# Top-32 attention and two feed-forward layers on one core: scores rewritten in place, divisions and norms moved to ScalarE, early heads parked in DRAM, and a new order

## The chip, the cores and the metric

One NeuronCore of one Trainium2 chip runs the whole program. The metric is device time of one execution in microseconds (us); lower is better. The engines are TensorE (PE; PEld is its weight load), VectorE (DVE), ScalarE (ACT), GpSimd (POOL) and SyncE (SP), which issues every DMA of this kernel from one in-order queue.

## The reference, cut to what matters

```python
B, H, S, D = 4, 8, 576, 64                 # attention; then d_model = 512, hidden 2048
scores = q @ k.T / sqrt(D)                 # per batch and head, 576 x 576
kth = 32nd largest score of each row
attn = softmax(scores where scores >= kth, else -1e9)
x = (attn @ v), heads side by side         # (4, 576, 512)

u = x + real(fft over seq of fft over d_model of x)
u = u + relu(norm(u) @ w_ch1) @ w_ch2      # first feed-forward (w1a, w2a in the kernel)
out = u + relu((norm(u) * g_ln) @ w_ch1') @ w_ch2'   # second feed-forward (w1b, w2b)
```

Inputs are float32; the kernel splits float32 operands into pairs of float16 (high part, low part) and multiplies high*high, high*low, low*high, so each product of the feed-forward layers is three matmuls.

## The kernel before

**Tiles.** A *score tile* is 128 query rows by 576 keys. Each of the 4 batches has 36 of them: 8 heads with 4 tiles each, and 4 tiles that hold the last 64 rows of two heads, 144 in all. The function `attend` makes one: matmuls into `ps`, a ScalarE copy to `s`, then on VectorE four `MAX8` (the eight largest of each row) with three `MATCH_REPLACE8` between them (each with a `MATCH_VALUE_LOAD`), which leaves the 32nd largest score in `mx`. Then ScalarE makes the masked exponential (Prelu with a huge slope, then Exp), rounds it to float16 (`p`), GpSimd writes the low part beside it, a DMA transposes `p` to `pt`, and 14 matmuls multiply it with the values `vt` into `xp`. After the four tiles of a head `evacuate` divides by the sum of the weights and writes the head's columns into the batch's buffers `xA` and `xB` (and `xC` for the 64-row tiles). `xp` is one buffer: the next head's products wait until it is emptied.

**A batch after its attention.** `fourier_rows` (once after heads 0, 7, 1, 6, once at the end) and `fourier_columns` add the transform to `xA`, `xB`, `xC`; `norm` takes mean and variance on VectorE, a power on GpSimd, applies them (`t2k<-xA,tiny`), and a DMA transposes the float16 pair into `unT`. `ffn` then runs 16 steps for two row tiles (A or B, 256 rows) or one (C, shared by two batches): 12 matmuls of 256 columns with `W1A` or `W1B` into `mm`, a ReLU into `h`, and 6 matmuls per pair of row tiles of 512 columns into `acc`. The second layer's `w2b` comes from DRAM (`ws<-W2D`), step by step. At the end `xA`, `xB`, `xC` go out; B goes through two DMA transposes and a GpSimd copy that turn its rows round.

**Buffers.** `xA` and `xB` exist twice, so batch 2 can write its first head only when batch 0 has left the second feed-forward and its rows are on their way out; batch 3 waits for batch 1 in the same way. `s` exists three times, the exponential `e` twice, the scratch `t2k` three times.

**Weights and statistics.** The weights arrive as 64-bit words and are converted on ScalarE, VectorE and GpSimd (`W1A`, `W2A`, `W2F`, `W1B`), scaled by a power of two and split. `stats(b)` loads q, k and v of batch b piece by piece, lets TensorE form sums of squares, and `find_scales` makes the batch's scales `sc`, without which `prep` (load, scale, split, transpose q and k) can't begin. Batch 0's scores are computed in float32.

**What sets the order.** `Program.record` only notes operations. `Program.order` then places them: it keeps a clock for each engine and takes again and again the operation that can start first by the prices of `price`; among operations that could start alike the lower priority number wins. That number is `LEVELS[stage][engine]`, a table with five numbers for each named stage (`st`, `a`, `p`, `f`, `m`, `n`, `w...`), and then the order of writing. `PACE` gives the earliest times of loads of weights and statistics. The result is a fixed order for each engine and a fixed buffer for each tile; on the chip each engine works through its list in that order and waits where it must. The scheduler emits everything on one line, so all rows of the profile have line 427.

The batch loop sets stage names around `stats(b+1)`, `attention(b+1)`, `first_ffn(b, ...)`, `front(b+1)` and `second_ffn(b, ...)`: the feed-forward layers of batch b are mixed with the attention of batch b+1 wherever the planner sees room.

## Time and profile before

| | us |
|---|---|
| median of 3 runs (lowest to highest) | 1364.93 (1363.99 to 1368.43) |
| the profiled execution | 1367.71 |
| its span, first to last instruction | 1365.9 |
| TensorE busy | 1196.4 (88%) |
| VectorE busy | 1028.4 (75%) |
| ScalarE busy | 796.2 (58%) |
| GpSimd busy | 676.6 (50%) |
| weight loads on TensorE (PEld) | 749.4 (55%) |
| mean granted TensorE clock | 0.939 of full speed |

Busy times count an engine's instructions, neighbours overlap a little. An instruction's duration in the trace is longer than its share of the engine's time: the next one starts before it has ended. Where a cost is taken from a timeline, it is the distance between two starts. Matmul ends are modelled, so a stretch in which TensorE is busy isn't one in which it runs at its peak.

### The profile page before, as it was taken

To read this page: it belongs to the slowest core of one execution; us is meant where nothing else is said; L and a number is where in the kernel's file an instruction comes from. 1 tells how busy PE (TensorE), PEld (TensorE's weight loads), DVE (VectorE), ACT (ScalarE), POOL (GpSimd) and SP (SyncE) were. 2 spreads that over 40 slices of the span, in tenths; PEclk is the share of its full clock that TensorE was granted. 3 is DMA by queue.
4 is the path that set the end of the run, shared out by engine and by line. 5 is a ranking of instruction groups with operands and counts; after the bars stand their busy time and mean duration, and the time that the engine had idled before them with its cause. 6 is when DMAs were issued, how large, how long until landed. Compare 5 with 4: busy or idle time off the path is not lost. (4 is left out here: it accounts for less than half of the span.)

```text
span 1365.9 us, 27326 instructions
## 1 busy us (share of the span) xinstructions
PE 1196.4 (88%) x9422; PEld 749.4 (55%) x9422; DVE 1028.4 (75%) x2597; ACT 796.2 (58%) x1741; POOL 676.6 (50%) x1015
## 2 busy tenths in 40 slices
PE   6787887577788779989999999979999999999995
PEld 3343434333555446656666666656666666666663
DVE  5989898978999898499599996968999751322221
ACT  3569696577786986466667664667676541212111
POOL 3566344545786874576667546656664441101000
PEclk9998787578899979999999999999999999999999
DMA  6898637767866457777454675895545735002346
GB/s 176 228 269 217 165 76 237 188 179 184 202 145 138 86 107 171 198 140 166 96 111 73 122 154 117 192 203 113 97 78 102 163 77 120 17 9 70 116 108 155
DMA packets 349430, 190.11 MB, mean 139 GB/s; under 512 B 288617, under 2 KB 306154, under 8 KB 349162
## 3 DMA queue, kind: packets, MB, share of 16 engines
q1 hardware_dynamic: 349290, 188.35, 59.5%
q8 instruction: 74, 1.21, 0.4%
q14 instruction: 66, 0.54, 0.1%
HBM read 108.07 MB, written 13.11 MB: 89 GB/s over the span
## 5 line engine op out<-in xcount | busy, mean ns | idle before, releaser
L427 DVE MAX8 mx<-w 128x8 f32<-128x576 f32 x432 | 315.6, 748 | 2.4
L427 ACT ACTIVATE h<-mm 128x256 f16<-128x256 f32 (+1 forms) x320 | 114.7, 358 | 307.7 <-PE mm L427 250.6
L427 POOL TENSOR_TENSOR p<-e,p 128x512 f16<-128x512 f32 (+1 forms) x288 | 207.4, 738 | 96.1 <-ACT p L427 76.9
L427 PEld LDWEIGHTS <-h 128*128 128x128 f16 x1728 | 160.6, 98 | 161.1 <-issue 26.3
L427 PE MATMUL acc<-ws,h 128*128 128x512 f16 x864 | 223.3, 383 | 18.1 <-DMA ws<-W2D 17.5
L427 PE MATMUL mm<-unT,W1B 128*128 128x256 f16 (+1 forms) x1920 | 225.0, 264 | 10.7 <-ACT W1B L427 5.4
L427 PE MATMUL mm<-unT,W1A 128*128 128x256 f16 (+1 forms) x1920 | 226.1, 264 | 2.9 <-DMA unT<-t2k 2.8
L427 PE MATMUL acc<-W2A,h 128*128 128x512 f16 x864 | 221.5, 380 | 5.1 <-POOL h L427 2.9
L427 POOL TENSOR_TENSOR h<-hr,h 128x256 f16<-128x256 f32 (+1 forms) x224 | 143.2, 642 | 151.1 <-ACT hr L427 76.0
L427 PEld LDWEIGHTS <-W1B 128*128 128x128 f16 (+1 forms) x1984 | 177.4, 99 | 72.8 <-issue 10.0
L427 PEld LDWEIGHTS <-W1A 128*128 128x128 f16 (+1 forms) x1984 | 178.2, 99 | 70.0 <-POOL W1A L427 10.6
L427 DVE MATCH_REPLACE8 w<-mx,w 128x576 f32<-128x576 f32 x288 | 213.0, 740 | 0.0
L427 DVE SCALAR_TENSOR_TENSOR h<-mm,h 128x256 f16<-128x256 f32 (+1 forms) x96 | 36.3, 378 | 166.5 <-ACT h L427 146.7
L427 ACT ACTIVATE e<-s,tiny 128x576 f32<-128x576 f32 x144 | 110.6, 774 | 60.3 <-DVE tiny L427 58.3
L427 PEld LDWEIGHTS <-pt 128*128 128x128 f16 (+1 forms) x2240 | 95.7, 106 | 70.3 <-DMA pt<-p 43.7
L427 PE MATMUL xp<-vt,pt 128*128 128x65 f16 (+1 forms) x2240 | 106.9, 203 | 28.0 <-DMA pt<-p 27.2
L427 DVE MAX8 mx<-s 128x8 f32<-128x576 f32 x144 | 107.5, 747 | 28.9 <-ACT s L427 28.8
L427 PE MATMUL ps<-kt,qt 128*128 128x64 f16 (+4 forms) x512 | 89.5, 323 | 28.5 <-ACT s L427 27.0
L427 DVE MATCH_REPLACE8 w<-mx,s 128x576 f32<-128x576 f32 x144 | 106.6, 740 | 0.0
L427 ACT ACTIVATE p<-e 128x576 f16<-128x576 f32 x144 | 97.8, 682 | 5.6 <-DMA pt<-p 5.5
L427 ACT ACTIVATE s<-ps 128x576 f32<-128x576 f32 x144 | 92.7, 644 | 12.1 <-PE ps L427 11.7
L427 ACT ACTIVATE e<-e,tiny,sc 128x576 f32<-128x576 f32 x108 | 93.0, 864 | 0.9
(152 smaller groups left out, 1565.6 us busy)
## 6 DMA issues: line engine op xcount, KB each, us to landing
ws<-W2D SPq DMA_DIRECT2D x160, 256.0 KB
W1B<-in_moe_w_ch_dram SPq DMA_DIRECT2D x56, 512.0 KB
n<-in_q_dram SPq DMA_DIRECT2D x32, 128.0 KB
n<-in_k_dram SPq DMA_DIRECT2D x32, 128.0 KB
n<-in_v_dram SPq DMA_DIRECT2D x32, 128.0 KB
W2F<-W1B SPq DMA_DIRECT2D x16, 256.0 KB
ws<-in_moe_w_ch_dram SPq DMA_DIRECT2D x16, 256.0 KB
W1B<-W2F SPq DMA_DIRECT2D x16, 256.0 KB
```

Source lines behind the costliest of these rows:

```text
L427: getattr(getattr(self.nc, op.eng), op.method)(*[fix(a) for a in op.args], **{k: fix(v) for k, v in op.kw.items()})
```

## The change

- `attend`: Prelu and Exp write over the score tile `s` itself, so the buffers `e` go away and `s` exists four times. The mask takes the 32nd largest score straight from `mx` (scale -1, small slope, and a second scale `nc` in Exp), so the small VectorE operation that negated it goes away, one in each of 144 tiles.
- `evacuate`: the division by the sum of weights is done on ScalarE for all batches (before: for batch 0). One VectorE operation for two tiles becomes two ScalarE operations.
- `norm`: for the pairs in `NACT` (batch, layer) the normalisation itself is a ScalarE operation with scale and bias, and one more small VectorE operation a tile makes the bias. These are 27 of 36 tiles.
- `evacuate_head`, `bring_back`: batches 2 and 3 write their first four heads (0, 7, 1, 6) to a scratch tile and by DMA to DRAM (`XD`); before the first Fourier rows they are read back into `xA` and `xB`, which are claimed only then.
- `stats`: pieces of 256 instead of 512 columns, through a buffer of their own (`sq`, one), no longer through `t2k`, which exists four times now.
- New stage names, new `LEVELS` and `PACE`, and other prices in `price`: so the order of every engine's instructions is new.

```diff
-EVACT = (0,)
+EVACT = (0, 1, 2, 3)
+NACT = ((0, 1), (1, 0), (1, 1), (2, 0), (2, 1), (3, 0))
...
-PACE = {'1a': (7.0, 4.0, 20.0, 15.5), '2a': (21.0, 4.5, 0.0, 14.5), '2b': (76.0, 10.0, 92.0, 13.0), '1b': (0.0, 26.5, 364.0, 0.0), 's1': (26.0, 9.5, 230, 0.5), 's2': (193.0, 22.0, 670, 8.0), 's3': (72.0, 48.0, 100, 2.5)}
+PACE = {'1a': (8.0, 1.5, 85.0, 4.5), '2a': (2.0, 4.0, 159.0, 0.0), '2b': (67.0, 1.0, 246.0, 0.0), '1b': (13.0, 16.5, 98.0, 34.0), 's1': (1.0, 5.5, 230, 0.5), 's2': (107.0, 3.5, 670, 8.0), 's3': (2.0, 3.5, 100, 2.5)}
...
-            op.cost = (130 if psum else 70) + n / (1.92 if fast else 0.96)
+            fields = sum(isinstance(op.kw.get(k), View) for k in ("scalar", "scalar1", "scalar2"))
+            op.cost = (133 if op.method == "match_replace" else 66) + 57 * fields + n / (1.92 if fast else 0.96)
...
-        nb = tiny(2)
-        c = scale(b, "c")
-        sm.tensor_scalar(out=nb[:, 0:1], in0=mx[:, 31:32], scalar1=-1.0, scalar2=None, op0=ALU.mult)
-        sm.tensor_scalar(out=nb[:, 1:2], in0=mx[:, 31:32], scalar1=mx[:, 0:1], scalar2=c, op0=ALU.subtract, op1=ALU.mult)
-        e = P.tile("e", [128, 576], F32)
-        act.activation(out=e, in_=s, func=AF.Prelu, bias=nb[:, 0:1], alpha=BIG)
-        act.activation(out=e, in_=e, func=AF.Exp, scale=c, bias=nb[:, 1:2])
+        nb = tiny(1)
+        sm.tensor_scalar(out=nb, in0=mx[:, 31:32], scalar1=mx[:, 0:1], scalar2=scale(b, "c"), op0=ALU.subtract, op1=ALU.mult)
+        act.activation(out=s, in_=s, func=AF.Prelu, scale=-1.0, bias=mx[:, 31:32], alpha=1.0 / BIG)
+        act.activation(out=s, in_=s, func=AF.Exp, scale=scale(b, "nc"), bias=nb)
...
+        if "A" not in x:
+            t = P.tile("t2k", [128, 4, 64], F32)
+            evacuate(b, xp[:, 0:260].rearrange("p (a c) -> p a c", a=4), 4, slice(0, 128), [(0, 4, t)])
+            if not away.get(b):
+                away[b] = (P.tile("XD", [4, 128, 256], F32), [])
+            d, heads = away[b]
+            sp.dma_start(out=d[len(heads)], in_=t.rearrange("p a c -> p (a c)"))
+            heads.append(h)
+            return
...
+            if on_act:
+                nm = mv[:, 10 + j:11 + j]
+                dve.tensor_scalar(out=nm, in0=mv[:, 2 * j:2 * j + 1], scalar1=mv[:, 6 + j:7 + j], scalar2=-1.0, op0=ALU.mult, op1=ALU.mult)
+                act.activation(out=un, in_=u, func=AF.Identity, scale=mv[:, 6 + j:7 + j], bias=nm, claim=unT)
```

**Place 1: VectorE, the first normalisation of batch 0** (`t2k<-xA`, two tiles; TensorE's first feed-forward matmul needs both). `W1B<-W1B` and `W1B<-ws` convert weights of the second layer; `MAX`, `MATCH_REPLACE` belong to score tiles of batch 1. Before:

```order
L427 MATCH_REPLACE w_176<-mx_128,w_176 128x576
L427 TENSOR_SCALAR W1B_91<-W1B_91 128x512
L427 TENSOR_SCALAR t2k_221<-xA_196,tiny_115 128x512
L427 SCALAR_TENSOR_TENSOR W1B_91<-W1B_91 128x512
L427 TENSOR_SCALAR t2k_220<-xA_196,tiny_115 128x512
L427 MAX mx_128<-w_176 128x8
```

Changed:

```order
L429 TENSOR_SCALAR t2k_223<-xA_196,tiny_122 128x512
L429 TENSOR_SCALAR tiny_116<-tiny_116 128x2
L429 MAX mx_131<-w_182 128x8
L429 MAX mx_128<-w_181 128x8
L429 TENSOR_SCALAR tiny_117<-mx_131,sc_272 128x1
L429 MATCH_REPLACE w_181<-mx_128,w_181 128x576
L429 MAX mx_129<-s_175 128x8
L429 MAX mx_128<-w_181 128x8
L429 MATCH_REPLACE w_182<-mx_129,s_175 128x576
```

The second normalisation (beyond this piece) stands 15 rows after the first now, not 2. Ahead of it, 42 score tiles were begun before and 47 are now.

**Place 2: VectorE, the end of batch 1's attention** (`sc_268` before, `sc_273` and `sc_274` now are the scales of the next batches; `xA<-acc` takes up the second feed-forward of batch 0; `t2k<-mm,nident` begins `find_scales`). Before:

```order
L427 MAX mx_131<-w_177 128x8
L427 TENSOR_SCALAR tiny_115<-mx_131 128x1
L427 TENSOR_SCALAR tiny_115<-mx_131,sc_267 128x1
L427 SCALAR_TENSOR_TENSOR xA_196<-acc_256,desc_111,xA_196 128x512 x2
L427 TENSOR_SCALAR tiny_116<-xp_246,sc_267 64x2
L427 TENSOR_SCALAR tiny_124<-xp_246,sc_267 128x4
L427 RECIPROCAL tiny_116<-tiny_116 64x2
L427 RECIPROCAL tiny_124<-tiny_124 128x4
L427 TENSOR_TENSOR xC_207<-xp_246,tiny_116 64x128
L427 TENSOR_TENSOR t2k_222<-mm_250,nident 128x384
```

Changed:

```order
L429 TENSOR_TENSOR tiny_116<-tiny_116,cmul 128x3 x2
L429 MAX mx_131<-w_182 128x8
L429 COPY sc_273<-tiny_116 128x2
L429 COPY sc_274<-tiny_123 128x2
L429 COPY sc_274<-tiny_123 128x1 x2
L429 TENSOR_SCALAR tiny_121<-mx_131,sc_272 128x1
L429 COPY sc_273<-tiny_116 128x1 x2
```

The scales of batches 2 and 3 are made ahead of the batch's last divisions now, and the feed-forward result `xA<-acc` is taken up three score tiles later.

**Place 3: SP, early heads of batch 2** (changed alone; before there was none of it). `XD` is the scratch in DRAM, `pt<-p` the transposed weights of a score tile, `out_dram<-xB` the rows of batch 0:

```order
L429 DMA XD_266<-t2k_223 128x256
L429 DMA out_dram<-xB_201 128x512
L429 DMA xA_196<-XD_266 128x2x64
L429 DMA_TRANSPOSE xB_201<-t2k_221 128x8x128
L429 DMA_TRANSPOSE pt_192<-p_187 128x9x128
```

The second early head leaves for DRAM before batch 0's rows have left `xB`; each batch has four such writes and eight reads in this queue.

## Rows read from the trace of the kernel before

**Rows 1.** Windows by stage: stretch, length, busy us (count) of engines, clock, DMA, GB/s.
```profile
0.00:348.00 348.00, 256.08 (x1425) 129.25 (x1426) 303.35 (x748) 237.44 (x460) 174.00 (x237) 0.83 0.74 194
348.00:573.00 225.00, 196.21 (x1697) 126.91 (x1697) 194.95 (x505) 167.11 (x370) 153.49 (x224) 0.94 0.65 145
573.00:847.00 274.00, 258.66 (x2311) 170.08 (x2310) 240.19 (x612) 176.72 (x406) 168.94 (x277) 0.99 0.60 124
847.00:1084.00 237.00, 218.02 (x1952) 144.33 (x1951) 214.33 (x530) 156.68 (x349) 140.89 (x228) 0.99 0.65 132
1084.00:1366.00 282.00, 267.46 (x2043) 178.82 (x2041) 75.55 (x205) 58.27 (x160) 39.27 (x50) 0.99 0.35 88
```

**Rows 2.** Timeline of TensorE: first feed-forward matmul; steady feed-forward; the last steps.
```profile
348.19 0.80 PE L427 MATMUL mm<-unT,W1A 128*128 128x256 f16 x3 [2.27 <-DMA unT<-t2k]
...
1161.41 1.47 PE L427 MATMUL mm<-unT,W1A 128*128 128x256 f16 x12
1162.72 1.46 PE L427 MATMUL acc<-W2A,h 128*128 128x512 f16 x6
1164.01 1.47 PE L427 MATMUL mm<-unT,W1A 128*128 128x256 f16 x12
...
1339.25 2.63 PE L427 MATMUL acc<-ws,h 128*128 128x512 f16 x6 [2.03 <-DMA ws<-W2D]
```

**Rows 3.** Timeline of VectorE, batch 2's first head: start, us, operation, idle before.
```profile
661.93 0.34 DVE L427 TENSOR_SCALAR tiny<-xp,sc 64x2 f32<-64x2 f32 x2 [10.54 <-PE xp L427]
...
662.58 0.27 DVE L427 TENSOR_TENSOR xA<-xp,tiny 128x128 f32<-128x128 f32 x1
662.78 0.27 DVE L427 TENSOR_TENSOR xB<-xp,tiny 128x128 f32<-128x128 f32 x1
...
663.16 0.13 DVE L427 TENSOR_SCALAR tiny<-mx 128x1 f32<-128x1 f32 x1
663.22 0.25 DVE L427 TENSOR_SCALAR tiny<-mx,sc 128x1 f32<-128x1 f32 x1
...
667.77 0.76 DVE L427 MAX8 mx<-s 128x8 f32<-128x576 f32 x1 [4.06 <-ACT s L427]
```

**Rows 4.** Timeline of VectorE, batch 3's first head.
```profile
891.33 0.22 DVE L427 TENSOR_SCALAR tiny<-xp,sc 128x4 f32<-128x4 f32 x1 [3.07 <-PE xp L427]
...
896.96 0.76 DVE L427 MAX8 mx<-s 128x8 f32<-128x576 f32 x1 [4.42 <-ACT s L427]
```

**Rows 5.** Timeline of VectorE, from one batch's attention to the next, and the last search.
```profile
552.11 1.41 DVE L427 SCALAR_TENSOR_TENSOR xA<-acc,desc,xA 128x512 f32<-128x512 f32 x2 [6.36 <-PE acc L427]
...
565.89 0.43 DVE L427 TENSOR_TENSOR t2k<-xA,xB 128x257 f32<-128x257 f32 x1 [4.25 <-PE mm L427]
...
822.15 0.56 DVE L427 TENSOR_TENSOR t2k<-mm,nident 128x384 f32<-128x384 f32 x1 [3.60 <-PE mm L427]
...
1084.02 0.76 DVE L427 MAX8 mx<-w 128x8 f32<-128x576 f32 x1
```

**Rows 6.** Timeline of VectorE, the first normalisation of batch 0.
```profile
333.14 0.54 DVE L427 TENSOR_SCALAR t2k<-xA,tiny 128x512 f32<-128x512 f32 x1
333.60 0.69 DVE L427 SCALAR_TENSOR_TENSOR W1B<-W1B 128x512 int32<-128x512 int32 x1
334.20 0.54 DVE L427 TENSOR_SCALAR t2k<-xA,tiny 128x512 f32<-128x512 f32 x1
```

**Rows 7.** Groups by line and shape: count, busy us, mean ns, idle before.
```profile
L427 DVE TENSOR_SCALAR tiny<-mx 128x1 f32<-128x1 f32 x180 | 24.5, 151 | 0.7
L427 ACT ACTIVATE W1A<-W1A,wsc 128x512 f16<-128x512 f32 x16 | 11.5, 721 | 1.4 <-PE mm L427 1.3
L427 ACT ACTIVATE xA<-xp,tiny 128x64 f32<-128x64 f32 x16 | 4.0, 304 | 0.0
```

**Rows 8.** Waits of VectorE from 348 to 1084: us in total, times, longest.
```profile
DVE mx L427 <- ACT s L427: 25.5, 14, 4.5
DVE tiny L427 <- PE xp L427: 23.4, 12, 10.5
```

More of the change, by code (lines that the diff above doesn't have):

```diff
@@ L399, in order @@
                 path = max(t + op.lat, path) + op.move
-                op.end = path + 1570
+                op.end = path + 650
                 moved.append(op.end)
@@ L470, in tile_attention_fourier_ffn @@
         P.tag(name, 2048 * banks, bufs, space=PSUM)
-    for name, shape, dt in (("W2F", [16, 128, 512], F32), ("W2D", [16, 128, 2, 512], F16)):
-        P.tag(name, 0, space=DRAM, shape=shape, dtype=dt)
+    for name, bufs, shape, dt in (("W2F", 1, [16, 128, 512], F32), ("W2D", 1, [16, 128, 2, 512], F16), ("XD", 2, [4, 128, 256], F32)):
+        P.tag(name, 0, bufs, space=DRAM, shape=shape, dtype=dt)
     def tiny(n, dt=F32):
@@ L514, in find_scales @@
             dve.scalar_tensor_tensor(out=sc[:, 2:3], in0=t[:, 3 * n:3 * n + 1], scalar=0.125, in1=t[:, 3 * n + 1:3 * n + 2], op0=ALU.mult, op1=ALU.mult)
-            dve.tensor_scalar(out=sc[:, 3:4], in0=sc[:, 2:3], scalar1=-1.0, scalar2=None, op0=ALU.mult)
+            dve.tensor_scalar(out=sc[:, 3:4], in0=sc[:, 2:3], scalar1=-BIG, scalar2=None, op0=ALU.mult)
         if "v" in names:
@@ L522, in scale @@
     def scale(b, nm, pr=slice(0, 128)):
-        if b in F32B and nm in ("sq", "sk", "c"):
-            return 0.125 if nm == "c" else 1.0
+        if b in F32B and nm in ("sq", "sk", "c", "nc"):
+            return {"c": 0.125, "nc": -0.125 * BIG}.get(nm, 1.0)
         return scales[b][pr, SC[nm]]
@@ L561, in stats @@
         for i, x in enumerate((q, k, v)):
-            for c in range(5):
-                n = 512 if c < 4 else 256
+            for c in range(9):
                 t0, step = PACE[f"s{b}"][:2]
-                P.at(t0 + (5 * i + c) * step, (f"s{b}", 0, 5 * i + c))
-                t = P.tile("t2k", [128, 512], F32)
-                sp.dma_start(out=t[:, 0:n], in_=flat(x, b)[:, c * 512:c * 512 + n])
-                gram(ps[:, i, :], t[:, 0:n], n, c == 0, c == 4)
+                P.at(t0 + (9 * i + c) * step, (f"s{b}", 0, 9 * i + c))
+                t = P.tile("sq", [128, 256], F32)
+                sp.dma_start(out=t, in_=flat(x, b)[:, c * 256:c * 256 + 256])
+                gram(ps[:, i, :], t, 256, c == 0, c == 8)
         P.at(0)
@@ L876, in evacuate, with bring_back @@
             dve.tensor_tensor(out=o, in0=xv[:, j:j + m, 0:64], in1=den[pr, j:j + m].spread([rows, m, 64]), op=ALU.mult)
+    away = {}
     def evacuate_head(b, h, xp):
         x = xbuf[b]
+        if "A" not in x:
[7 more added lines that the diff above has]
+            return
         evacuate(b, xp[:, 0:260].rearrange("p (a c) -> p a c", a=4), 4, slice(0, 128),
                  [(j, 2, x[nm][:, :, h * 64:(h + 1) * 64]) for nm, j in (("A", 0), ("B", 2))])
+    def bring_back(b):
+        x = xbuf[b]
+        x["A"] = P.tile("xA", [128, 2, 512], F32)
+        x["B"] = P.tile("xB", [128, 2, 512], F32)
+        d, heads = away[b]
+        for i, h in enumerate(heads):
+            for nm, j in (("A", 0), ("B", 128)):
+                sp.dma_start(out=x[nm][:, :, h * 64:(h + 1) * 64], in_=d[i, :, j:j + 128].rearrange("p (a c) -> p a c", a=2))
     def attention(b):
@@ L896, in attention @@
                 if not x:
-                    x["A"] = P.tile("xA", [128, 2, 512], F32)
-                    x["B"] = P.tile("xB", [128, 2, 512], F32)
+                    if b < 2:
+                        x["A"] = P.tile("xA", [128, 2, 512], F32)
+                        x["B"] = P.tile("xB", [128, 2, 512], F32)
                     x["C"] = xbuf[b - 1]["C"] if b % 2 else P.tile("xC", [128, 512], F32)
@@ L1018, in norm @@
             un = P.tile("t2k", [128, 512], F32)
[L1019 to L1020 removed]
+            if on_act:
+                nm = mv[:, 10 + j:11 + j]
+                dve.tensor_scalar(out=nm, in0=mv[:, 2 * j:2 * j + 1], scalar1=mv[:, 6 + j:7 + j], scalar2=-1.0, op0=ALU.mult, op1=ALU.mult)
+                act.activation(out=un, in_=u, func=AF.Identity, scale=mv[:, 6 + j:7 + j], bias=nm, claim=unT)
+            else:
+                dve.tensor_scalar(out=un, in0=u, scalar1=mv[:, 2 * j:2 * j + 1], scalar2=mv[:, 6 + j:7 + j], op0=ALU.subtract, op1=ALU.mult,
+                                  claim=unT)
             o = P.tile("t2k", [128, 2, 512], F16)
@@ L1133, in front @@
         fourier_rows(b, 1)
+        P.phase("fft", f"c{b}")
         fourier_columns(b)
+        P.phase("fft", f"g{b}")
         do_norm(b, "A", 0)
```

31 lines of the change are left out of this document (17 added, 14 removed), and 5 rows, old and new, of the table mhalf.

## The prediction

> **What bounds the kernel now.** I read the windows by stage first [rows 1], with two cuts: where TensorE's first feed-forward matmul starts, 348.2 us [rows 2], and where VectorE's last top-32 search starts, 1084.0 us [rows 5]. The reader is to see three regimes. Up to 348 TensorE is busy 256 of 348 us, at a granted clock of 0.83 of full speed (so part of it at 1.2 GHz), and VectorE 303 of 348: converting weights and searching score tiles sets the pace. From 348 to 1084 both are nearly full: VectorE 649 of 736 us (195+240+214), TensorE 673 (196+259+218). From 1084 TensorE is busy 267 of 282 us and VectorE 76: only feed-forward work is left. The end of the program is therefore where VectorE has finished the attention, plus the feed-forward work that TensorE then still has in hand. I make the sum in that form and check it against TensorE's idle time, which is 92 us before 348, 63 between and 15 in the tail.
>
> Next I read the waits of VectorE in the middle [rows 8], and then their places in the timelines [rows 3 to 5]. The long ones stand at the seams between batches: 10.5 and 4.1 us at batch 2's first head, 3.1 and 4.4 at batch 3's, which ends for want of free `xA` and `xB`; 6.4 and 4.2 between batches 1 and 2, 3.6 between 2 and 3, where VectorE waits for a feed-forward result, for Fourier input, and for the statistics that must precede the next batch's scales.
>
> **VectorE's share of the removed work.** Three edits, priced by distances between starts. The negation of the 32nd score: 663.16 to 663.22 is 0.06 us [rows 3], by 144 is 8.6 us. The division: 662.58 to 662.78 is 0.20 us [rows 3]; batches 1 to 3 have 60 of these (24 on `xA`, 24 on `xB`, 12 on `xC`), 12 us. The normalisation: 333.14 to 333.60 is 0.46 us [rows 6], less 0.06 for the new small operation that makes the bias, 0.40; 22 of the 27 tiles lie ahead of the last search (batch 3's five come later), 8.8 us. Together 29 us. By whole busy times it would be more: 24.5 us for 180 negations and their like [rows 7] is 0.136 each, 19.6 for 144; 0.27 by 60 is 16; 0.54 less 0.13 by 22 is 9; 45 us. Since VectorE's instructions overlap, I take 29 and keep 45 for the range. The new `nc` scale costs nothing: it takes the place of another small multiplication, once a batch.
>
> **What ScalarE takes on.** 120 divisions of 64 columns at 0.30 us [rows 7] are 37 us, and 27 normalisations at about 0.72, the price of a 512-column copy with a scale operand [rows 7], are 19 us: 56 us more on an engine that is busy 500 of the 736 middle microseconds and 58 of 282 in the tail [rows 1]. Nothing on its side says it can't be hidden; what it can lengthen is the 25.5 us that VectorE waits for `s` [rows 8]. I set nothing for it and keep 0 to 12, half of that row again. The Trainium skill speaks against these two moves (ScalarE: Activation LUTs, section Rules for kernel authors): additions and multiplications belong on VectorE, which is faster per element. The rows agree on the price, 0.27 us for two tiles there against 0.61 here; by the rule the moves lose 25 us of engine time (56 less 16 and 15), and that would enter the sum only where ScalarE sets the pace.
>
> **Buffers.** Exponential in place: before, a tile held one of three `s` until the mask and one of two `e` until GpSimd had written the low part; now it holds one of four `s` throughout. Five buffers became four. A search is seven operations of some 0.7 us (0.76 for one that stands alone [rows 5]), 5 us a tile; two tiles are interleaved, one is being filled and one is in ScalarE's and GpSimd's hands: just enough. If GpSimd is late, VectorE has no next tile. No row shows it. The nearest is the mean wait for `s`, 25.5/14 = 1.8 us [rows 8]: none to six more of these, 0 to 10 us, and I take 3.
>
> **What the parking of early heads frees.** The waits at the first heads of batches 2 and 3 sum to 22.1 us (10.54+4.06+3.07+4.42) [rows 3, 4]; with nothing to wait for but a scratch tile, they go: I take all of it. Against it stand 8 writes and 16 reads in SP's queue, each read behind a write on which it waits, with transposes of `p` queued behind (place 3). No row shows such a pair; a score tile that comes late costs VectorE 4.1 to 4.4 us [rows 3, 4], and two such are 8. Score tiles run two ahead of the search, so I take 0, up to 8.
>
> **What the new order moves.** Two counts from the order matter. First, at the last matmul of scores TensorE has left 987 feed-forward matmuls of 256 columns and 600 of 512 before, 1104 and 672 now. A group of 12 takes 1.31 us and a group of 6 takes 1.29 [rows 2], so the tail grows by 117/12 x 1.31 + 72/6 x 1.29 = 12.8 + 15.5 = 28 us. The tail's own shape, its last waits for `ws` included [rows 2], is the same in both orders. Second, ahead of the second normalisation of batch 0 (place 1) VectorE has 5 more score tiles begun (18 MAX8 and 14 replacements more), 6 more conversion pairs and 5 half ones: at 0.7 us each for the 32, 0.46 and 0.60 (333.60 to 334.20 [rows 6]) for a pair and half of that for the small ones, some 31 us, less the negations that are gone: about 30. So the first feed-forward matmul comes up to 30 us later, and with it TensorE's idle time before it grows. This is the same work drawn forward, no loss for VectorE; it is one for TensorE if it can't make it up.
>
> At the seams the scales come ahead (place 2), the statistics go through their own buffer, and the feed-forward result that VectorE waited 6.4 us for is taken up three tiles later. Of the 14.2 us of long waits there (6.36+4.25+3.60) [rows 5] I take half, 7: the Fourier chain is a chain still.
>
> **TensorE's check.** Between first feed-forward matmul and last search TensorE has 28 us of feed-forward less, and some 5 us of score tiles went ahead: 640 of the 673 busy us. The idle share in that stretch was 13% from 348, 6% from 573 and 8% from 847 [rows 1]. With the first matmul at 378 and 9% as before the search would end at 378 + 640/0.914 = 1078, with 6% at 1056, and some 10 us earlier still if the clock of the first part were 0.99 instead of 0.94 [rows 1]. The VectorE sum gives 1084 - 29 - 22 - 7 + 3 = 1029. The two disagree by 17 to 50 us, so TensorE will hold VectorE back, in waits for `s` and `xp`: 0 to 50 us. I take 15, near the lower end, because busy time also counts TensorE's gaps between dependent matmuls: weight loads fill 63% of the saturated tail and 62% from 573, but only 56% from 348 and 61% from 847 [rows 1], so there is room inside the busy stretches. [...]
>
> **The sum.** The profiled execution took 1367.7 us (span 1365.9), 2.8 above the median. 1367.7 - 29 (VectorE work) - 22 (parked heads) - 7 (seams) + 3 (buffers) + 28 (tail) + 15 (TensorE holds back) = 1356 for such an execution; the search would end at 1044. Against the median that is 1356 - 2.8 = **1353 us**, 0.9% below 1364.9. With the bounds: all savings at their upper end and nothing held back, 1367.7 - 45 - 22 - 14 + 28 - 2.8 = 1312; 50 held back with ScalarE, buffers and queue at their worst, 1367.7 - 29 - 22 + 12 + 10 + 8 + 28 + 50 - 2.8 = 1422, for which everything would have to go wrong at once.
>
> **The rivals.**
> *Slower: the late start of the feed-forward decides.* If TensorE keeps its 9% idle from 378 on, the search ends at 1078, and 1078 + 282 + 28 = 1388 of span, 1387 on the median's scale. It decides as soon as the middle's TensorE idle share stays above some 6%, when the search ends after 1060. For it: TensorE was near full in every stage, and the work moved off VectorE isn't TensorE's. Against: 92 of its 170 idle us lie ahead of 348 and the seams' waits were VectorE's at a time when TensorE had filling work.
> *Nothing changes.* VectorE's 29 us less, the freed 22 and the 28 us longer tail, with 23 to 31 held back, end within 4 us of 1365: 1338 + 27. For it: work removed and tail added cancel almost to the microsecond.
> *ScalarE's burden shows.* It makes every `s` that the search reads and empties `xp`; with 0.61 us for a pair of divisions in place of 0.27 [rows 3, 7] and more in its queue, the 25.5 us of waits for `s` [rows 8] double: 1353 + 25 = 1378. The Trainium skill's rule named above points this way. Against: it is idle a third of the middle.
> *Faster by more.* VectorE sets the pace alone (the sum's 1029) and the 45 us hold: 1084 - 45 - 22 - 14 = 1003, + 282 + 28 = 1313 of span, 1312 on the median's scale. For it: the granted clock would rise with fewer gaps, the seams empty.
>
> **How the numbers follow.** Forecast (faster, near 1353, from 1338 to 1360) 0.42; faster by more 0.15; nothing changes 0.15; late feed-forward 0.20; ScalarE 0.08. A measurement here tells 0.3% from no change, 4 us: faster 0.57, same 0.15, slower 0.28. The range leaves out the lower half of the faster case and the worst of the slower ones: 1325 to 1386.
>
> **What would show it.** VectorE busy near 995 us in all and ScalarE near 850 if the edits do what they say; no wait for `xp` above 5 us at the first heads of batches 2 and 3; the first feed-forward matmul between 360 and 385; the last search near 1040 and a tail of 310 us with TensorE busy 95% of it. The prediction is wrong if the last search comes after 1060 (TensorE holds back more, look at waits for `s` and at its idle from 378 on), if SP's queue stands on reads of `XD`, or if the waits for `s` grow beyond 50 us.

## The result and the profile after

The changed kernel took 1353.92 us (median of 5 runs, 1351.23 to 1357.19) against 1364.93 (1363.99 to 1368.75) before: a ratio of 0.9911, 95% interval 0.9886 to 0.9936. The chips differ by up to 0.4% for one kernel (before: 1359.9 to 1364.9), so all that follows compares ratios to the kernel before on the same chip; on the chip of some later runs the changed kernel came to 0.9917 (0.9892 to 0.9942). One of the nine executions of the later kernel e8_midboth took 2266 us and is left out of its ratio.

A trace is of one execution, and that one can lie some us from its median: 2.8 above it for the kernel before (1367.7), 2.7 below for the changed kernel (1351.2), 1.5 above for its second trace (1354.6), 9 above for e4 further on. Windows of different traces carry these differences.

The busy times of the engines after, the page's first part (share of the span, instructions):

```profile
PE 1186.2 (88%) x9422; PEld 744.4 (55%) x9422; DVE 999.9 (74%) x2393; ACT 841.7 (62%) x1888; POOL 684.6 (51%) x1015
```

VectorE was forecast near 995 and ScalarE near 850. The marks of the forecast (answering [rows 2 to 5]): first, from TensorE's timeline, the first feed-forward matmul (start, us, operation, idle before); then, from VectorE's, the seam behind batch 1, the first evacuation of batch 2 and of batch 3, the largest wait at a parked head, two late waits for scores, the last search.

```profile
365.61 1.65 PE L429 MATMUL mm<-unT,W1A 128*128 128x256 f16 x7 [1.10 <-DMA unT<-t2k]
```
```profile
540.10 0.48 DVE L429 TENSOR_SCALAR tiny<-xp,sc 64x2 f32<-64x2 f32 x2 [7.48 <-PE xp L429]
...
594.15 0.22 DVE L429 TENSOR_SCALAR tiny<-xp,sc 128x4 f32<-128x4 f32 x1 [0.49 <-PE xp L429]
...
834.01 0.20 DVE L429 TENSOR_SCALAR tiny<-xp,sc 128x4 f32<-128x4 f32 x1
...
897.53 0.22 DVE L429 TENSOR_SCALAR tiny<-xp,sc 128x4 f32<-128x4 f32 x1 [3.45 <-PE xp L429]
...
1005.34 0.76 DVE L429 MAX8 mx<-s 128x8 f32<-128x576 f32 x1 [7.06 <-ACT s L429]
...
1017.18 0.76 DVE L429 MAX8 mx<-s 128x8 f32<-128x576 f32 x1 [4.50 <-ACT s L429]
...
1044.52 0.76 DVE L429 MAX8 mx<-w 128x8 f32<-128x576 f32 x1
```

The waits of 10.5, 4.1, 3.1 and 4.4 us at the first heads [rows 3, 4] are gone. New ones stand elsewhere. The waits of VectorE from 365.6 to 1044.5 (in total, times, longest), which answer [rows 8]:

```profile
DVE mx L429 <- ACT s L429: 36.9, 16, 7.1
DVE tiny L429 <- PE xp L429: 20.7, 12, 7.5
```

They are 58 us for 49 before. The groups of ScalarE's score copy, before and then after (busy, mean, idle time before them and what ended it), show a wait that the forecast had named as possible (Buffers) but had no row for:

```profile
L427 ACT ACTIVATE s<-ps 128x576 f32<-128x576 f32 x144 | 92.7, 644 | 12.1 <-PE ps L427 11.7
```
```profile
L429 ACT ACTIVATE s<-ps 128x576 f32<-128x576 f32 x144 | 93.7, 650 | 39.1 <-PE ps L429 21.1 <-POOL p L429 15.4 <-PE acc L429 1.0
```

With the exponential in place and the new order, ScalarE waits for GpSimd (`p`, 15.4 us) before it may copy new scores. What the four buffers cost in the old order is a matter for an experiment, below.

Where the time went is read best from windows cut at the first score tile of batches 1, 2 and 3 (the first MAX8 that reads `s`), the last search and the end. Before, and then after (stretch, length, busy us of PE, PEld, DVE, ACT, POOL, clock, DMA, GB/s):

```profile
0.00:279.90 279.90, 209.19 (x1158) 108.22 (x1158) 247.83 (x610) 187.85 (x356) 138.22 (x179) 0.83 0.73 193
...
279.90:573.60 293.70, 243.70 (x1970) 148.32 (x1969) 250.92 (x644) 217.29 (x475) 189.73 (x283) 0.90 0.68 157
573.60:846.80 273.20, 257.86 (x2306) 169.61 (x2305) 239.54 (x610) 175.92 (x405) 168.32 (x275) 0.99 0.60 124
846.80:1084.00 237.20, 218.22 (x1954) 144.41 (x1953) 214.53 (x531) 156.88 (x350) 141.04 (x229) 0.99 0.65 132
1084.00:1365.90 281.90, 267.46 (x2043) 178.82 (x2041) 75.55 (x205) 58.27 (x160) 39.27 (x50) 0.99 0.35 88
```
```profile
0.00:265.50 265.50, 208.52 (x1160) 106.97 (x1160) 243.41 (x574) 185.60 (x351) 146.03 (x177) 0.86 0.74 200
...
265.50:544.90 279.40, 219.74 (x1853) 135.13 (x1853) 248.68 (x594) 225.08 (x498) 183.41 (x272) 0.90 0.70 165
544.90:783.10 238.20, 225.90 (x2024) 148.43 (x2024) 215.35 (x511) 181.54 (x428) 161.12 (x269) 1.00 0.65 131
783.10:1044.50 261.40, 245.13 (x2207) 162.02 (x2205) 218.43 (x509) 180.12 (x425) 147.51 (x239) 0.99 0.64 130
1044.50:1349.50 305.00, 286.93 (x2181) 191.88 (x2180) 74.01 (x209) 69.40 (x188) 46.55 (x61) 0.99 0.37 90
```

Batches 0 and 1 became 14.4 and 14.3 us shorter (15.3 and 11.1 in the second trace of the changed kernel). The last three windows together became longer, 792.3 to 804.6 us, and they grew by what TensorE has to do in them, 743.5 to 758.0: feed-forward work that no longer lies in the second window lies there now (117 matmuls fewer in the second, 109 more in the last three). In these windows TensorE is busy 92 to 95% of the time before and after. So the gain, 16.4 us between these two executions (11.0 between the medians), is 28.7 in the first two batches less 12.3 behind them.

### The profile page after: what moved, and what is told of

It is laid out like the page before. It is cut to its first block, busy times and chain, and to the rows that moved or that the text cites. A ratio compares the mean times of both kernels' runs of the same rounds, so it can differ in the third digit from the quotient of the medians.

```text
span 1349.5 us, 27275 instructions
## 1 busy us (share of the span) xinstructions
PE 1186.2 (88%) x9422; PEld 744.4 (55%) x9422; DVE 999.9 (74%) x2393; ACT 841.7 (62%) x1888; POOL 684.6 (51%) x1015
## 5 line engine op out<-in xcount | busy, mean ns | idle before, releaser
L429 POOL TENSOR_TENSOR p<-s,p 128x512 f16<-128x512 f32 (+1 forms) x288 | 209.0, 743 | 100.1 <-ACT p L429 71.8
L429 PE MATMUL acc<-ws,h 128*128 128x512 f16 x864 | 219.8, 381 | 22.7 <-DMA ws<-W2D 19.8
L429 PE MATMUL mm<-unT,W1B 128*128 128x256 f16 (+1 forms) x1920 | 220.0, 262 | 2.4 <-ACT h L429 1.9
L429 ACT ACTIVATE s<-s,mx 128x576 f32<-128x576 f32 x144 | 111.6, 776 | 34.8 <-DVE mx L429 31.8
L429 PE MATMUL ps<-kt,qt 128*128 128x64 f16 (+5 forms) x512 | 91.0, 312 | 21.6 <-ACT s L429 17.5
L429 ACT ACTIVATE p<-s 128x576 f16<-128x576 f32 x144 | 98.3, 686 | 7.0 <-DMA pt<-p 6.3
L429 ACT ACTIVATE s<-s,tiny,sc 128x576 f32<-128x576 f32 x108 | 93.0, 872 | 9.7 <-DVE tiny L429 9.2
```

What stands on the lines that cost most here:

```text
L429: getattr(getattr(self.nc, op.eng), op.method)(*[fix(a) for a in op.args], **{k: fix(v) for k, v in op.kw.items()})
```

## The experiments

Theory V is the prediction's sum: VectorE's work sets the end of attention. Its rivals: TensorE or the order sets the pace and the edits count for nothing (T, P), or ScalarE's load costs (A, S). In the later kernels (e9 to e11) A stands for something else: three engines are equally full. In the kernels below operations are exchanged after the order was fixed: what runs around them, the buffers and every other instruction's place stay. In the code, `op.sub` lists what is issued in an operation's place; an empty list leaves it out. This table has the ratio with its interval and, from the profiled execution, the lengths of the five windows as cut above:

| kernel | ratio to before | batch 0 | 1 | 2 | 3 | tail |
|---|---|---|---|---|---|---|
| before | 1 | 279.9 | 293.7 | 273.2 | 237.2 | 281.9 |
| after | 0.9911 (0.9886-0.9936) | 265.5 | 279.4 | 238.2 | 261.4 | 305.0 |
| after, again | 0.9917 (0.9892-0.9942) | 264.6 | 282.6 | 238.4 | 261.4 | 305.8 |
| e1_oldops | 1.0037 (1.0022-1.0051) | 270.3 | 289.1 | 241.5 | 264.0 | 302.8 |
| e2_divnorm | 1.0001 (0.9990-1.0013) | 263.1 | 289.3 | 240.2 | 263.8 | 303.4 |
| e3_newops | 1.0091 (1.0064-1.0119) | 273.6 | 294.3 | 274.3 | 239.4 | 283.4 |
| e4_inplace4 | 1.0004 (0.9986-1.0022) | 281.0 | 295.0 | 271.6 | 235.3 | 284.0 |

**The order and parking without the edits of operations.** In the changed kernel, with what its order fixes (the negation's result is read by nothing here, it only takes VectorE's time):

```diff
+        op.sub = [("vector", "tensor_scalar", (), dict(out=nb2[:, 0:1], in0=mx[:, 31:32], scalar1=-1.0, scalar2=None, op0=ALU.mult)),
+                  (op.eng, op.method, op.args, op.kw)]
...
-                    act.activation(out=o[:, i, :], in_=xv[:, j + i, 0:64], func=AF.Copy, scale=den[pr, j + i:j + i + 1])
+                    op = act.activation(out=o[:, i, :], in_=xv[:, j + i, 0:64], func=AF.Copy, scale=den[pr, j + i:j + i + 1])
+                    if b:
+                        op.sub = [] if i else [("vector", "tensor_tensor", (), dict(out=o, in0=xv[:, j:j + m, 0:64], in1=den[pr, j:j + m].spread([rows, m, 64]), op=ALU.mult))]
...
+                op.sub = []
+                op = act.activation(out=un, in_=u, func=AF.Identity, scale=mv[:, 6 + j:7 + j], bias=nm, claim=unT)
+                op.sub = [("vector", "tensor_scalar", (), dict(out=un, in0=u, scalar1=mv[:, 2 * j:2 * j + 1], scalar2=mv[:, 6 + j:7 + j], op0=ALU.subtract, op1=ALU.mult))]
```

> The changed kernel with its order, buffers and parked heads as they are, and only the three edits of operations undone: the negation is back (180 on VectorE), the division and the norms are back on VectorE (so VectorE gets about 29 us more, ScalarE about 56 us less). Theory V, the prediction's sum: VectorE's work sets the end of attention, so at least two thirds of 29 us come back: 1373 to 1383 us. Rival T: order and TensorE set the pace, the edits only made VectorE wait more: 1350 to 1358 us, with the last MAX8 at about the same time (1045) and VectorE's waits shorter. Rival A: the 56 us that ScalarE gained were a burden: below 1350 us.

It is 0.4% slower than the kernel before: the new order, its buffers and the parking, which this run doesn't take apart, bring nothing with the old operations in them. (The order was planned for the new operations; one planned for the old ones might do better and was not tried.) The edits of operations, in this order, bring 1.0037 - 0.9911 = 1.26%, 17 us for 29 priced. On the scale of the first comparison it would be 1370 us, 3 below V's range and 12 above T's: theory V, somewhat cheaper. Windows of this kernel for batches 1 to 3:

```profile
270.30:559.40 289.10, 224.47 (x1851) 137.20 (x1852) 259.43 (x650) 215.12 (x453) 183.47 (x271) 0.89 0.68 159
559.40:800.90 241.50, 226.74 (x2029) 148.84 (x2028) 224.90 (x560) 169.99 (x386) 162.53 (x269) 1.00 0.62 130
800.90:1064.90 264.00, 247.91 (x2225) 162.92 (x2222) 228.78 (x562) 169.00 (x378) 149.19 (x240) 0.99 0.62 131
```

VectorE has 10.7, 9.6 and 10.4 us more here than in the changed kernel, and the windows are 9.7, 3.3 and 2.6 us longer: nearly the full price in batch 1's (6.5 against the second execution of the changed kernel), a third and less where TensorE is busy 94%. The last search comes 20.4 us later (17.9 than in the second trace). This trace is of a long execution, 1369.5 us where the median is 1364.7, so the distances are upper ends; the 17 us by the ratios are the firmer number.

VectorE's waits for `s` between first feed-forward matmul and last search, here and then in the next kernel, and the score copy's group here:

```profile
DVE mx L432 <- ACT s L432: 33.5, 19, 6.9
```
```profile
DVE mx L432 <- ACT s L432: 34.0, 17, 6.7
```
```profile
L432 ACT ACTIVATE s<-ps 128x576 f32<-128x576 f32 x144 | 93.0, 646 | 40.4 <-PE ps L432 21.8 <-POOL p L432 15.6 <-PE acc L432 1.6
```

ScalarE has 38 us less to do here (803.4 us busy against 841.7), yet most of the longer waits remain: 33.5 us for 36.9 in the changed kernel and 25.5 before. So they come mostly with the new order and its buffers, as does ScalarE's wait for GpSimd (15.6 us), and not with ScalarE's new operations.

**Division and norms alone.** The last two edits of that diff, the negation staying out.

> The changed kernel with only the softmax division of batches 1 to 3 and the norms back on VectorE (about +21 us of VectorE, -56 us of ScalarE), order and buffers untouched. Theory V: 1366 to 1375 us. Rival T (VectorE's operations count for nothing): 1350 to 1358 us. Rival A (ScalarE's load costs, the rule of the Trainium skill's page on it): 1340 to 1350 us, and VectorE's waits for s fall from 37 us in the middle stages to 25 or less.

Division and norms on VectorE cost 1.0001 - 0.9911 = 0.9%, 12 us for 20.8 priced, and the negation the rest of e1, 0.4% or 5 us for 8.6. On the first scale that is 1365 us, just below V's range and above T's, and rival A falls: with 39 us less on ScalarE (803.0 against 841.7 in all) it was slower, and the waits for `s` were 34.0 us, not 25 or less. The Trainium skill's rule that additions and multiplications belong on VectorE (ScalarE: Activation LUTs, Rules for kernel authors) is not borne out in this order, where VectorE's time is the dearer.

**The edits of operations without the order.** The same three edits made in the kernel before (`EVACT` of all batches, the negation out and the mask with `BIG` at 2^80, norms of the six on ScalarE), in its order, with `s` and `e` apart.

> The kernel before with its order and buffers (s and e apart, no parked heads), and only the three edits of operations: no negation, division and the six norms on ScalarE. Theory V: VectorE's 29 us less are the gain, two thirds of it or more: 1336 to 1346 us. Rival T: 1362 to 1368 us, the new order brought all of the change's gain. Rival A: ScalarE's extra 56 us make it slower, 1368 to 1380 us.

Not faster: 0.9% slower, as rival A had it. The same removal of VectorE work that is worth 17 us in the new order is worth nothing in the old. The trace is of one of its shorter executions (1366.9 us, median 1372.3), no longer than the trace of the kernel before, so it doesn't show the 0.9%: in it batch 0 is 6.3 us shorter, and each later window 0.6 to 2.2 us longer. Its waits of VectorE from 340 to 1082 us:

```profile
DVE mx L430 <- ACT s L430: 50.9, 23, 5.7
DVE tiny L430 <- PE xp L430: 22.2, 11, 8.1
```

The wait for `s` doubled from 25.5 [rows 8], as ScalarE's rival had it. All idle time of VectorE between first feed-forward matmul and last search went from 87 to 116 us, by about the 29 us that the edits took away, and the last search came 2.4 us earlier. A reading, not shown alone: the old places don't suit the new owners, as ScalarE now does the division and the norm at points of its queue which the old order chose for VectorE, with score copies behind them. How much of it is ScalarE's work and how much its place, this run doesn't separate; an order planned anew for these operations was not tried.

**The exponential in place.** The kernel before, order untouched, `s` and `e` in four shared buffers (one score copy moved behind the last use of its buffer).

```diff
+        tag.slots = (tag.slots + other.slots)[0:4]
...
+            b.tag = tag
+            a.slot = b.slot = k % 4
...
         e = P.tile("e", [128, 576], F32)
+        P.pairs.append((s.vt, e.vt))
```

A tile's `s` and `e` get the same one of four places here, `k % 4`.

> The kernel before with its order, its only difference that the exponential is written over the scores, in four buffers in place of three for scores and two for exponentials; no operation is added or taken. The prediction's term for this was +3 us, 0 to 10: 1365 to 1375 us. If the shared buffers are the source of the changed kernel's longer waits for scores (36.9 us for 25.5 in the middle stages), 1374 to 1382 us with ScalarE's score copies waiting for GpSimd; if they cost nothing, 1363 to 1367 us.

No cost (0.9986 to 1.0022). VectorE's waits for scores from 349 to 1083 us (the merged buffers carry both names) sum to 24.4 us for 25.5, and the mean wait for the copy did not grow:

```profile
DVE mx L452 <- ACT s L452: 19.7, 12, 4.5
...
DVE mx L452 <- ACT e L452: 4.7, 2, 4.4
```

So four buffers for five don't lengthen these waits in the old order. But ScalarE hardly waits for GpSimd here, 0.5 us named before its copies (two groups, by the buffer's name):

```profile
L452 ACT ACTIVATE s<-ps 128x576 f32<-128x576 f32 x108 | 69.6, 644 | 10.6 <-PE ps L452 9.6 <-PE mm L452 0.7
L452 ACT ACTIVATE e<-ps 128x576 f32<-128x576 f32 x36 | 23.3, 647 | 3.8 <-PE ps L452 3.2 <-POOL p L452 0.5
```

The 15.4 us of the changed kernel arise only in the new order, and what they cost there no run shows.

**Who sets the pace in batch 1.** There VectorE, TensorE and ScalarE work 162, 164 and 150 of 179 us (365.6 to 545). In the changed kernel, 20 score tiles (15 to 34) of batch 1 lose the last replacement and the last MAX8, or the mask and the exponential, and the first feed-forward network of batch 0 loses its high-by-low products.

> The changed kernel as it is, as the anchor of this group on its chip: 0.9886 to 0.9936 of the kernel before, first FFN matmul at about 366 us and last MAX8 at about 1045 us of its profiled execution.

It came as expected: 0.9917, 368.1 and 1047.0 us. It is the second measure beside the first in what follows.

```diff
+        less = b == 1 and 15 <= i <= 34
...
-            dve.max(out=mx[:, 8 * r:8 * r + 8], in_=src)
+            op = dve.max(out=mx[:, 8 * r:8 * r + 8], in_=src)
+            if less and r == 3:
+                op.sub = []
             if r < 3:
-                dve.match_replace(out=w, in_to_replace=mx[:, 8 * r:8 * r + 8], in_values=src, imm_value=NEG)
+                op = dve.match_replace(out=w, in_to_replace=mx[:, 8 * r:8 * r + 8], in_values=src, imm_value=NEG)
+                if less and r == 2:
+                    op.sub = []
```

> The changed kernel without the last of the four rounds of the top-32 search (the third MATCH_REPLACE and the fourth MAX8) in 20 score tiles of batch 1: about 28 us less of VectorE between 340 and 540 us, nothing else touched; the softmax there is not the reference's. Theory V (VectorE sets the end of attention): the last MAX8 comes 19 to 28 us earlier, and the time falls by 10 to 20 us, since part of it comes back as FFN work left behind the last search. Rival P (TensorE sets the pace of that stage): last MAX8 and time within 5 us of the changed kernel, VectorE stands 25 us longer on TensorE's results. Rival J (VectorE and TensorE are equally dense there, 17 and 16 us idle of 179): last MAX8 5 to 15 us earlier, time 0 to 8 us less.

```diff
                 for a, c in ((0, 0), (0, 1), (1, 0)):
-                    pe.matmul(out=hp[:, 0:N], lhsT=W1[:, dc, f // 8, a, fs], rhs=unT[:, c * 4 + dc, 0:N],
+                    op = pe.matmul(out=hp[:, 0:N], lhsT=W1[:, dc, f // 8, a, fs], rhs=unT[:, c * 4 + dc, 0:N],
                               start=(i == 0), stop=(i == 11))
+                    if less and c:
+                        op.sub = []
```

and the same in the second product.

> The changed kernel without the high-by-low products in the first FFN of batch 0, tiles A and B (4 of 12 matmuls of the first product and 2 of 6 per row tile of the second, about 28 us of TensorE between 366 and 560 us), nothing else touched; that FFN is less exact. Theory V: the last MAX8 stays within 5 us, and the time stays within 6 us of the changed kernel, TensorE being 28 us more idle in the middle. Rival P: last MAX8 15 us or more earlier, time 15 to 28 us less. Rival J: last MAX8 up to 10 us earlier, time 3 to 12 us less.

> The changed kernel with both cuts together: 28 us less of VectorE and 28 us less of TensorE in the middle of batch 1's attention. Theory V: about as the cut of VectorE alone, with a little more (last MAX8 25 to 28 us earlier, time 20 to 28 us less, as no work is left over for the tail). Rival P: as the cut of TensorE alone. Rival J: more than both cuts alone together, 20 to 28 us.

The cut of ScalarE, and the combinations:

```diff
-        act.activation(out=s, in_=s, func=AF.Prelu, scale=-1.0, bias=mx[:, 31:32], alpha=1.0 / BIG)
-        act.activation(out=s, in_=s, func=AF.Exp, scale=scale(b, "nc"), bias=nb)
+        op = act.activation(out=s, in_=s, func=AF.Prelu, scale=-1.0, bias=mx[:, 31:32], alpha=1.0 / BIG)
+        op2 = act.activation(out=s, in_=s, func=AF.Exp, scale=scale(b, "nc"), bias=nb)
+        if less:
+            op.sub = op2.sub = []
```

> The changed kernel without the first two of the three ScalarE passes of the softmax (the one that cuts below the 32nd score and the exponential) in 20 score tiles of batch 1: about 28 us less of ScalarE between 340 and 540 us, nothing else touched; the softmax there is not the reference's. ScalarE works 150 of 179 us in that stage, VectorE 162, TensorE 164. Theory S (ScalarE's queue sets the pace there, filled by the change): the first score tile of batch 2 comes 8 to 25 us earlier than 545 us. Theory A (three engines are equally full, each alone is cut in vain): 5 us or less. Rival L (the pace is that of the chain of one score tile and its buffers): 5 us or less as well.

> The changed kernel with the cut of VectorE (last round of the search) and the cut of ScalarE (two softmax passes) together in the same 20 tiles of batch 1, 28 us each; the softmax there is not the reference's. Theory S: as the cut of ScalarE alone or somewhat more, 10 to 28 us earlier. Theory A: 5 to 12 us earlier, TensorE then being what is left. Rival L: more than 20 us, since the two cuts also take 2.8 us out of every tile's chain.

> The changed kernel with all three cuts together, of VectorE, ScalarE and TensorE, about 28 us each in the stage 366 to 545 us; softmax and FFN there are not the reference's. Theory A: the first score tile of batch 2 comes 18 to 28 us earlier, as all three engines have 28 us less, and the time falls by 12 to 28 us. Theory S: as with ScalarE's cut alone. Rival L: as with the cuts of VectorE and ScalarE.

Measured (the changed kernel: 0.9911 and 0.9917, batch 1's window 279.4 and 282.6 us, last search 1044.5 and 1047.0):

| kernel | ratio to before | batch 1's window | first tile of batch 2 | last search |
|---|---|---|---|---|
| e6_midvector | 0.9882 (0.9855-0.9909) | 279.2 | 542.2 | 1040.8 |
| e7_midtensor | 0.9924 (0.9895-0.9954) | 287.7 | 552.1 | 1053.6 |
| e8_midboth | 0.9923 (0.9896-0.9949) | 282.4 | 546.9 | 1050.7 |
| e9_midscalar | 0.9903 (0.9878-0.9928) | 278.3 | 543.3 | 1041.3 |
| e10_midvecsca | 0.9881 (0.9855-0.9907) | 279.5 | 543.4 | 1041.9 |
| e11_midall | 0.9884 (0.9854-0.9914) | 276.2 | 539.0 | 1041.2 |
| e12_midallq | 0.9847 (0.9824-0.9869) | 272.9 | 534.1 | 1035.8 |

The windows are from one execution each, and the two traces of the changed kernel differ by 3.2 us in batch 1; e7's is the longest of its six (1359.3 us, median 1352.9). No theory got its numbers throughout. The windows of batch 1 in e6 and in e11 show that the work is gone (VectorE 249 to 224 and 223 us, ScalarE 225 to 199, TensorE 220 to 203) and the length is not:

```profile
263.00:542.20 279.20, 222.45 (x1853) 137.15 (x1853) 224.22 (x533) 225.89 (x498) 182.38 (x272) 0.88 0.71 165
```
```profile
262.80:539.00 276.20, 202.66 (x1661) 117.17 (x1661) 222.90 (x533) 199.04 (x458) 182.08 (x272) 0.88 0.73 167
```

e6 came out as rival J: on its chip the time fell by 6.5 us between medians (1353.1 to 1346.6; the intervals of the two ratios overlap), and the last search came 6.2 us earlier. Theory V, which held for adding VectorE's work, fails for taking more away: 25 us less there shorten batch 1 by 0 to 3 us and the run by about 5. In e7 the time stayed (1352.9), near theory V, but the search came 6.6 us later; rivals P and J fail. e8 is like e7, as rival P had worded it, though P's own number had failed in e7: with TensorE's cut on top, e6's gain is gone (0.9923 for 0.9882). Theory S falls with e9, 2 to 4 us at the first tile of batch 2, where A and L had 5 or less. In e10 it is 2 to 4 us as well, less than any of them. Theory A wanted 18 to 28 us of e11 and got 6 to 8. Part of that is where the cuts lie: VectorE's left-out operations stood from 394 to 520 us in the changed kernel, ScalarE's from 398 to 522, TensorE's from 367 to 495, so the three overlap for 100 us only.

**The loads for the scales as well.** In the timeline of SP's queue the gaps between issues from 366 to 480 sum to only 25 of 114 us, and the loads of 128 KB for batch 3's scales, 26 of the 27, stand in it and share one buffer. The rows of that timeline merge neighbours, though: by single instructions the gaps are 39 us in the changed kernel, so the queue was less full than I read. In SP's waits from 366 to 1045, 9 with 9.9 us in all are for one of these loads to land.

```diff
-                sp.dma_start(out=t, in_=flat(x, b)[:, c * 256:c * 256 + 256])
+                op = sp.dma_start(out=t, in_=flat(x, b)[:, c * 256:c * 256 + 256])
+                if b == 3:
+                    op.sub = []
```

> The kernel with all three cuts (VectorE, ScalarE and TensorE, about 28 us each, in the middle of batch 1), and the 27 loads of 128 KB that the scales of batch 3 are summed from left out as well, which stand in SP's queue from 382 to 473 us, each waiting in that queue for the one buffer; the sums are taken over what the buffer holds, so batch 3's scales are not the reference's either. Theory Q (in that stretch SP's queue, of which only 25 of 114 us are free, and the single buffer set the pace once the engines are lighter, or already before): the first score tile of batch 2 comes before 530 us (545 in the changed kernel, 539 with the three cuts), the time is 1320 to 1338 us if before is at 1363. Rival L (the chain of one score tile through its buffers): it stays at 535 to 542 us, the time at 1341 to 1350 us.

Nearer to rival L: 1341 us is in its range and outside Q's, and the first tile of batch 2 at 534.1 is 0.9 us ahead of L's range and 4 behind Q's. That is 4.9 us earlier than e11, not the 9 that theory Q wanted. In its timelines of VectorE and TensorE one sees where part of the gained time ends up, at the last value product of batch 1:

```profile
529.29 0.48 DVE L432 TENSOR_SCALAR tiny<-xp,sc 64x2 f32<-64x2 f32 x2 [12.59 <-PE xp L432]
```
```profile
515.76 2.23 PE L432 MATMUL mm<-unT,W1B 128*128 128x256 f16 x19
517.84 0.60 PE L432 MATMUL xp<-vt,pt 128*128 128x65 f16 x14
518.27 0.60 PE L432 MATMUL mm<-unT,W1B 128*128 128x256 f16 x4
518.71 2.75 PE L432 MATMUL acc<-ws,h 128*128 128x512 f16 x12
521.30 2.24 PE L432 MATMUL mm<-unT,W1B 128*128 128x256 f16 x19
...
524.67 0.60 PE L432 MATMUL xp<-vt,pt 128*128 128x65 f16 x14
...
528.17 1.08 PE L432 MATMUL xp<-vt,pt 128*64 128x65 f16 x28 [0.92 <-DMA pt<-p]
```

VectorE is through at 516.7 and stands 12.6 us for `xp`; it stood 7.5 there in the changed kernel, 11.4 in e6 and 13.4 in e11. TensorE's queue puts feed-forward matmuls of the second network (not cut) between the value products, and it is busy nearly all that time. But the last product itself started only when its transpose had landed (the 0.92 us of the last row, 1.04 in e11): there the chain of the last score tile, from its exponential to `pt`, ended last, by a microsecond. In the changed kernel TensorE came to that product without a gap. Some 4 to 6 us of a saving of VectorE in batch 1 are handed to this wait. What sets the pace between 366 and 480 is not settled: cuts of three engines and of SP's queue together took off 6.5 to 9.7 us. Single tiles' chains through `ps`, `p`, `pt` and `xp` were not tried alone, nor was GpSimd, which no cut made lighter, nor the rest of SP's queue.

## Why the prediction was right, step by step

**The form of the sum.** "Where VectorE has finished the attention, plus the feed-forward work that TensorE then still has": last search forecast at 1044, measured 1044.5; tail 310, measured 305.0 with TensorE busy 94%; first feed-forward matmul at 365.6, inside 360 to 385. Rival "late feed-forward decides" needed a search end after 1060 and a middle TensorE idle share above 6%; the share was 6.5% (44 of 679 us) and the end came at 1044. That rival lost on its price: TensorE was not as idle as it had been (8.6%), though its share was over the threshold that I gave. The threshold was worked out for a start at 378 and 640 us of work; the start came 12 us sooner and the work was 635 us, so the same 6.5% gives 365.6 + 635/0.935 = 1044.

**Where luck came in.** The forecast of 1353 against 1353.9 is closer than its terms. By e1 the operations brought 17 us where 29 stood, and order, buffers and parking cost 5 us (1.0037) where 17 stood (-22 - 7 + 3 + 28 + 15): each is 12 too high, and the two cancel. With the 15 that TensorE holds back set against the operations they are 14 and 2, nearer, but the sum didn't say where the 15 belong. The trace, besides, is of a short execution: its span of 1349.5 us lies 4 to 5 under the 1354 of the terms (1044 + 310).

**VectorE's 29 us.** Net of the part of the 15 us that TensorE holds back, the sum had 14 to 29 for this; e1 says 17 in time and 17.9 to 20.4 at the last search. The size held, the mechanism only half: e3 shows that it is no price of the operations alone, but of operations and order together, and e6 that 25 us more, taken from one batch, bring about 5.

**ScalarE's 56 us at nothing.** By busy times they were 45.5 (796.2 to 841.7). For this order e2 bears out that they cost less than the time they save VectorE, and e9 that ScalarE's load is not what sets the pace in batch 1; that they cost nothing is not shown. In the old order (e3) the rival's doubled wait for `s` came about, with 0.9% more time and not the 1.8% of its 25 us. What the forecast missed is that this rival hangs on the order.

**Buffers, +3.** e4: nothing in the old order (interval -1.9 to +3.0 us). The wait of ScalarE for GpSimd that the term feared is there in the new order, 15.4 us; e4 had 0.5 of it, so its price is open.

**Parking 22 and seams 7, tail +28.** The waits went, as forecast, but e1 shows what they were worth. With the old operations the last search came 19.1 us earlier (1084.0 to 1064.9) where 29 were summed, the tail grew by 20.9, and the time rose by 0.4%. The windows point to why: in batches 2 and 3 TensorE had 34 us of idle time in 510 before and has 31 in 505 in e1, so removing VectorE's waits there could hardly shorten them. Read so, the waits (-22 and -7) and the tail (+28) were not separate effects, as I wrote them, but one: feed-forward work pushed behind the last search. That these terms cancelled was not reasoned out, it was luck. In the changed kernel the tail grew by 23.1, not 28. The rival "nothing changes" is close to what e1 is.

**TensorE holds back 15.** All terms ahead of the tail, without the +3 that was none, sum to 58; the last search moved 39.5; so 18.5 were held back. That is a remainder, no measured wait: it takes up whatever the other terms had wrong. VectorE's waits for `s` and `xp` grew by 9 us (49 to 58). The choice near the lower end fits; its reason, room in the busy stretches, was not tested.

**The waits forecast.** No wait for `xp` above 5 us at the first heads: 0.49 and none, 3.45 at the largest of the parked ones. Waits for `s` 36.9, below the 50 that would have told against it. SP's queue stood 2.9 us for writes of `XD` in all.

## What to carry to other kernels

A step on a full engine has two prices, one for adding it and one for taking it away, and they hold only in the order around it: 29 us of VectorE work were worth 17 us in one order and less than nothing in the other, and 25 more, taken from one batch, about 5. Before crediting a removed wait, read TensorE's idle time of that window: here it was 34 of 510 us, and the removed waits came back as work behind the last search. Judge reordered kernels by windows cut at the same work (first tile of each batch), not at the same time, and see first how far each traced execution lies from its median.

## What the runs showed of the chip

In the traced execution of e7, with TensorE work taken away, the rest of it ran slower for a while. From 456 to 501 us the granted clock was 0.89, where the changed kernel had 1.00, and the same matmuls took longer. That window in e7, in the changed kernel (its second trace) and in e8, with the clock as the third number from the end:

```profile
456.00:501.00 45.00, 36.67 (x289) 20.91 (x290) 40.88 (x99) 39.90 (x90) 31.52 (x42) 0.89 0.43 86
```
```profile
456.00:501.00 45.00, 39.38 (x350) 25.18 (x347) 42.38 (x102) 41.31 (x91) 33.06 (x44) 1.00 0.46 88
```
```profile
456.00:501.00 45.00, 35.44 (x321) 21.30 (x317) 35.02 (x83) 41.93 (x94) 32.58 (x44) 0.97 0.44 89
```

Groups by shape in it, e7 and then the changed kernel (count, busy us, mean ns):

```profile
L432 PE MATMUL acc<-W2A,h 128*128 128x512 f16 x40 | 13.0, 418 | 2.6 <-ACT h L432 2.2 <-POOL h L432 0.3
...
L432 PE MATMUL mm<-C,unT 128*128 128x320 f16 x12 | 3.4, 372 | 0.0
```
```profile
L429 PE MATMUL acc<-W2A,h 128*128 128x512 f16 x60 | 15.8, 380 | 2.0 <-ACT h L429 2.0
...
L429 PE MATMUL mm<-C,unT 128*128 128x320 f16 x12 | 2.6, 298 | 0.0
```

At 0.89 the engine was part of the time at the lower of its two levels, 1.2 GHz. In the 90 us ahead of that it had been busy 68 us, 83 in the changed kernel. This execution came 5 to 7 us later to batch 2; the median of e7 is that of the changed kernel (1352.9 and 1353.1 us). That the emptier stretch is the cause is not shown: e8, busy 67 us in the same 90 us, had 0.97, e11 with 70 us 0.96, and e12 with 70 us 1.00.

In the first 95 us the clock row can't be trusted. From 50 to 75 us it says 1.00 in one execution of the changed kernel and 0.50 in another, yet one value product takes 245 and 244 ns in them (for each execution the window and then a group from 40 to 60 us), and the first batch ended alike (265.5 and 264.6 us):

```profile
50.00:75.00 25.00, 17.92 (x85) 8.83 (x84) 24.32 (x61) 17.56 (x33) 17.91 (x19) 1.00 0.98 260
```
```profile
L429 PE MATMUL xp<-vt,pt 128*128 128x65 f16 x18 | 1.9, 245 | 0.0
```
```profile
50.00:75.00 25.00, 19.31 (x101) 9.76 (x99) 24.32 (x60) 17.96 (x33) 17.74 (x18) 0.50 0.97 258
```
```profile
L429 PE MATMUL xp<-vt,pt 128*128 128x65 f16 x27 | 2.9, 244 | 0.0
```

From 456 to 501 us, at 1.00, the same product took 193 ns. The first trace holds no record of the clock at all before 97 us, and the row counts such time as full clock; the trace of the kernel before has none before 100 us. So the 0.83 and 0.86 of the first windows are probably too high (0.70 up to 265 us in the trace that has the record), and the mean clocks of whole executions (0.939 before, 0.949 and 0.912 for the two of the changed kernel) say little about their times.
